# Low words of weights and folded weights: subtractions on the vector engine replaced by identity products in PSUM and by accumulating transfers

## The chip, the core and the metric

One core of a Trainium2 chip runs the whole program; the figure is device microseconds from a run's timing, and a profile of one execution gives every instruction's start and length. The core has a tensor engine (PE, matrix products into PSUM; PEld is its weight load), a vector engine (DVE), a scalar engine (ACT), GpSimd (POOL) and SyncE (SP); SP and POOL issue the DMA transfers here.

## The reference, cut to what matters

```python
a = softmax(phi over the sequence)               # per head, 576 tokens x 32 memories
k_m = a^T k ; v_m = a^T v                        # 32 x 64 per head
attn = softmax(q k_m^T / 8) ; out = attn v_m     # 8 batches, 8 heads, 64 columns a head
x = out, heads side by side                      # 4608 x 512
h = x @ w_in ; r = max(h, 0) ; y = (r * r) @ w_out   # w_in 512 x 2048, w_out 2048 x 512
```

The data is float32 and the products must keep more digits than one reduced product does. So the kernel writes each operand as a high word that the tensor engine takes in one pass (type float32r) and a low word, the rest, and sums three products: high by high, high by low, low by high.

## The kernel before, in words

**Work.** A batch has 576 tokens: 512 "main" ones in four blocks of 128, and 64 left over. `memory` makes the 32 memories of four heads, `scores` and `attention` make the attention weights `ath`, `atl` (high and low). The values are not multiplied by the attention weights first: `vw_alone` (first pair of batches, 16 calls) and `vw_step` (later pairs) fold the memories' values into 256 columns of `w_in`, and the result, split again into high and low, is the tile `V` (row names vw). `mm1` then makes h for 128 hidden columns of one batch (12 products in two PSUM tiles), squares the positive part into `gh` and `glo` (high and low); `mm2` multiplies these by `w_out` (12 products of 512 columns into the four `acc` tiles). One call of `mm1` and one of `mm2` is a step; there are 128 steps, numbered in `seq`: the first 32 take batch 0, 1, 1 and 0 by eights, then batches 2 to 7 follow with 16 each. `mm2_left` does the tokens left over, once per pair of batches.

**Weights.** They come as float32. `decode` loads 256 KB pieces (`raw`, 16 of `w_in` called wi, 16 of `w_out` called wo), takes the two halves of each float apart on the vector engine, and puts the high part and the low part into a pair of words: L320 to L325 prepare `W` (the coarse value) and `T` (the rest, scaled), L326 adds them, a copy (a helper's line, L258, on ACT or DVE) makes the high word, L335 subtracts it from the sum to make the low word. Pieces of `w_in` are also stored to HBM (L339) and loaded again later (`wi_again`).

**Folded weights.** In `vw_alone`, 12 products (L468) fill one PSUM bank with the fold, a copy takes the high word (ACT or DVE), and L476 on the vector engine subtracts it from PSUM for the low word. The bank has one tile (tag `pv`).

**Order.** Every operation is recorded with an estimated cost for each engine that may do it, and `Plan.order` plays a list schedule with these costs: it decides which engine takes an operation that has two, and in which order each engine's instructions stand. The order is fixed when the program is built; at run time an engine takes its instructions strictly in it and waits where an input is late. Transfers are issued on SP (loads) and POOL (stores of the first six batches and of `w_in`).

Of the kernel before, what the change touches and what calls it, by code (L numbers as in the profile page):

```python
# [11 lines left out]
F32 = mybir.dt.float32  # L12
# [7 lines left out]
P = 128  # L20
# [4 lines left out]

STEP = 5200
LEAD = 9000

# [22 lines left out]
class Plan:  # L51
# [57 lines left out]
    def order(self):  # L109
        for o in reversed(self.ops):  # L110
            cost = min(o.ways.values()) + o.lat + o.size / 180.0 + (1800 if o.size else 0)
            late = min((u.late for u in o.users), default=1e9)
            if o.cap is not None:
                late = min(late, o.cap)
            o.late = late - cost
# [17 lines left out]
        while len(out) < len(self.ops):  # L133
# [38 lines left out]
            if o.size:  # L172
                wire = max(wire, t + 600) + o.size / 180.0
                o.end = wire + 1400
            out.append(o)
# [9 lines left out]
def tt(n):  # L185
    return 110 + 1.04 * n


def ts(n):
    return 110 + 0.52 * n  # L190


def act(n):
    return 120 + 0.86 * n
# [10 lines left out]
def tile_attention_moe(  # L205
# [63 lines left out]
    ident = sb.tile([P, P], F32, tag="ident", name="ident", bufs=1)  # L269
    make_identity(nc, ident)  # L270
    ones = sb.tile([P, 1], F32, tag="ones", name="ones", bufs=1)
    nc.vector.memset(ones, 1.0)
# [30 lines left out]
    def decode(kind, j, h, room):  # L303
# [15 lines left out]

        vec({"DVE": 560}, lambda e: nc.vector.tensor_scalar(tf(), high().bitcast(F32), TOP, -TOP, ALU.min, ALU.max), [rk], [tk], lead=True)  # L320
        op({"ACT": act(ND)}, lambda e: nc.scalar.activation(tf(), tf(), AF.Copy, scale=2.0 ** -112), [tk], [tk], lead=True)
        vec({"DVE": ts(ND)}, lambda e: nc.vector.tensor_scalar(W(), high(), SIGN, None, ALU.bitwise_and), [rk], [wk], lead=True)
        vec({"DVE": tt(ND)}, lambda e: nc.vector.scalar_tensor_tensor(W(), T(), 3, W(), ALU.logical_shift_left, ALU.bitwise_or), [tk, wk], [wk], lead=True)
        vec({"DVE": ts(ND)}, lambda e: nc.vector.tensor_scalar(T(), W(), POWER, None, ALU.bitwise_and), [wk], [tk], lead=True)
        vec({"DVE": tt(ND)}, lambda e: nc.vector.scalar_tensor_tensor(tf(), low(), 2.0 ** -52, tf(), ALU.mult, ALU.mult), [rk, tk], [tk], lead=True)  # L325
        vec({"DVE": tt(ND)}, lambda e: ENG[e].tensor_add(wf(), wf(), tf()), [tk, wk], [wk], lead=True)  # L326
        if kind == "wi":
            t = wi[0, j, 0, h] = st([P, 2, 2, SL], F32R, "wi", f"wi0_{j}_{h}", 3)
            part = lambda x: t()[:, x].rearrange("p c f -> p (c f)")
        else:  # L330
            t = wo[2 * j + h] = st([P, 2, DM], F32R, f"W{j}{'ab'[h]}", f"wo{j}{h}")
            part = lambda x: t()[:, x]
        k0, k1 = ((t, (h, x) if kind == "wi" else x) for x in (0, 1))
        op({"ACT": act(ND), "DVE": ts(ND)}, lambda e: copy(e, part(0), wf()), [wk], [k0], lead=True, port={"DVE": True})
        vec({"DVE": tt(ND)}, lambda e: ENG[e].tensor_sub(part(1), wf(), part(0).bitcast(F32)),  # L335
            [wk, k0], [k1], lead=True)
        if kind == "wi":
# [121 lines left out]
    def vw_alone(s, bp):  # L459

        ts_ = [wi[0, s, bp if s < 4 else 0, hh] for hh in (0, 1)]
        vh, vl = VT[bp]
        pw = pt("pv", f"pvw0_{s}_{bp}")

        def mm(e, hh):
            for i, (l, r) in enumerate(((vh, 0), (vh, 1), (vl, 0))):
                for x in (0, 1):
                    nc.tensor.matmul(pw()[:, hh * SL:(hh + 1) * SL], l()[:, 2 * hh + x, :], ts_[hh]()[:, r, x, :],  # L468
                                     start=(i == 0 and x == 0), stop=(i == 2 and x == 1))

        for hh in (0, 1):
            op({"PE": 720}, lambda e, hh=hh: mm(e, hh), [ts_[hh], vh, vl], [pw], lead=True, lat=300)
        V = VW[bp, s]
        part = lambda x: V()[:, x].rearrange("p h f -> p (h f)")
        op({"ACT": act(2 * SL), "DVE": tt(2 * SL)}, lambda e: copy(e, part(0), pw()), [pw], [(V, 0)], lead=True)
        vec({"DVE": tt(2 * SL)}, lambda e: nc.vector.tensor_sub(part(1), pw(), part(0).bitcast(F32)), [pw, (V, 0)], [(V, 1)], port=None, lead=True)  # L476

# [97 lines left out]
    def mm1(g):  # L575
# [11 lines left out]
        for h in (0, 1):  # L587
            cs = TOK[h]
            n = cs.stop - cs.start
            p = pt("h", f"h{g}_{h}", 2)  # L590

            def mm(e, cs=cs, n=n, p=p):
                i = 0
                for l, x in ((0, ah), (0, al), (1, ah)):
                    for hh in (0, 1):
                        nc.tensor.matmul(p()[:, 0:n], V()[:, l, hh, c0:c0 + P], x()[:, hh, cs], start=(i == 0), stop=(i == 5))  # L596
                        i += 1

            op({"PE": 6 * (n * 0.4167 + 11)}, mm, [V] + [(x, (hh, h)) for x in (ah, al) for hh in (0, 1)], [p], lat=300)
            op({"ACT": act(n) - 30, "DVE": tt(n)}, lambda e, cs=cs, n=n, p=p: nc.scalar.activation(r()[:, cs], p()[:, 0:n], AF.Relu) if e == "ACT"  # L600
               else nc.vector.tensor_scalar(r()[:, cs], p()[:, 0:n], 0.0, None, ALU.max), [p], [(r, h)])  # L601
        op({"ACT": act(SM)}, lambda e: nc.scalar.activation(gh(), r()[:, 0:SM], AF.Square), [r], [gh])  # L602
        op({"ACT": act(LEFT)}, lambda e: nc.scalar.activation(G()[:, 0, lc], r()[:, SM:S], AF.Square), [r], [(G, (b % 2, 0))])  # L603
        op({"ACT": act(S), "DVE": tt(S)}, lambda e: nc.scalar.activation(r(), r(), AF.Square) if e == "ACT"  # L604
           else nc.vector.tensor_mul(r(), r(), r()), [r], [r], port=BOTH)  # L605
# [102 lines left out]
    memory(0, 1, ("W4a", "W5a"))  # L708
    attention(0, True)
    for j in range(4):  # L710
# [76 lines left out]
```

## Time and profile before

| what | value |
|---|---|
| median of 3 runs | 840.82 us (840.16 to 842.5) |
| profiled execution | 842.42 us, of which 840.7 us from first to last instruction |
| PE busy | 770.8 us (92%), granted clock 0.983 on average |
| DVE busy | 607.8 us (72%) |
| ACT busy | 352.0 us (42%) |
| POOL busy | 55.1 us (7%) |

Shares of the whole span mix stages: the first 230 us carry all 32 decoded pieces and 16 folds beside 24 steps; the rest has no decoding. A busy PE is not a PE at its peak, since a product's length in the trace is more than the distance to the next product's start when they follow each other.

### The profile page before, as it was taken

Reading aid. Unit: us, or ns where it says so; the run is one execution under the profiler, and the core shown is the slowest. Engines: PE = TensorE matmul, PEld = TensorE weight load, DVE = VectorE, ACT = ScalarE, POOL = GpSimd, SP = SyncE. Lnnn points to the kernel's source line nnn. Section 1 sums busy time; section 2 is a strip of 40 time slices with the busy share of each in tenths; the row PEclk is TensorE's granted clock in tenths of the full one; section 3 lists DMA queues with packets and bytes.
Section 4 is the critical chain, followed back from the end, with each engine's and each line's share of the span. In section 5 each row is a group of like instructions: output and inputs, shape, how many; then the busy total and the mean of one; then the engine's idle time right before and its main releaser. Section 6 shows DMA issues by size and latency. Waiting matters only on the chain. (4 is left out here: it accounts for less than half of the span.)

```text
span 840.7 us, 12898 instructions
## 1 busy us (share of the span) xinstructions
PE 770.8 (92%) x4756; PEld 646.7 (77%) x4756; DVE 607.8 (72%) x1346; ACT 352.0 (42%) x819; POOL 55.1 (7%) x91
## 2 busy tenths in 40 slices
PE   3468669999969999999999999999999999999995
PEld 2246558989758788888888788888888888888884
DVE  3889999999747886686788656686869566784540
ACT  1234446556324344453334434553335344542320
POOL 3102110221000010001000100001000100000000
PEclk9999989999989999999999999999999999999998
DMA  7847673546563753332344433322532433100001
GB/s 218 231 136 236 184 217 128 176 151 204 149 149 98 190 125 101 106 102 51 100 136 105 129 110 101 114 68 51 142 84 56 125 114 101 54 14 37 1 1 62
DMA packets 91073, 97.87 MB, mean 116 GB/s; under 512 B 24644, under 2 KB 77892, under 8 KB 91012
## 3 DMA queue, kind: packets, MB, share of 16 engines
q1 hardware_dynamic: 80292, 81.55, 33.5%
q0 software_dynamic: 10720, 15.52, 7.0%
q8 instruction: 37, 0.61, 0.3%
q14 instruction: 24, 0.20, 0.1%
HBM read 79.17 MB, written 17.83 MB: 115 GB/s over the span
## 5 line engine op out<-in xcount | busy, mean ns | idle before, releaser
L596 PE MATMUL h<-ath,vw 128*128 128x320 f32 (+1 forms) x1024 | 215.3, 304 | 11.9 <-ACT r L600 6.3
L626 PE MATMUL acc<-wo,gh 128*128 128x512 f32 x512 | 206.7, 404 | 0.1
L627 PE MATMUL acc<-wo,gh 128*128 128x512 f32 x512 | 204.2, 399 | 0.0
L596 PEld LDWEIGHTS h<-ath,vw 128*128 128x128 f32 x1024 | 173.7, 193 | 28.5 <-ACT r L600 8.4
L629 PE MATMUL acc<-wo,glo 128*128 128x512 f32 x512 | 160.7, 407 | 2.9 <-DVE glo L606 2.4
L496 DVE TENSOR_TENSOR vw<-pvw,vw 64x256 fp32r<-64x256 f32 x192 | 78.6, 420 | 66.9 <-ACT vw L258 65.2
L258 ACT CAST vw<-pvw 64x256 fp32r<-64x256 f32 (+1 forms) x205 | 74.8, 380 | 104.0 <-PE pvw L487 65.2
L626 PEld LDWEIGHTS acc<-wo,gh 128*128 128x128 f32 x512 | 98.1, 192 | 20.6 <-ACT gh L602 1.5
L596 PE MATMUL h<-atl,vw 128*128 128x320 f32 (+1 forms) x512 | 112.8, 301 | 0.2
L627 PEld LDWEIGHTS acc<-wo,gh 128*128 128x128 f32 x512 | 98.2, 192 | 18.3
L601 DVE TENSOR_SCALAR r<-h 128x320 f32<-128x320 f32 (+1 forms) x142 | 65.0, 459 | 63.0 <-PE h L596 61.5
L629 PEld LDWEIGHTS acc<-wo,glo 128*128 128x128 f32 x512 | 89.6, 189 | 23.9 <-DVE glo L606 9.2
L602 ACT ACTIVATE gh<-r 128x512 fp32r<-128x512 f32 x128 | 80.8, 631 | 51.5 <-DVE r L601 39.1
L606 DVE TENSOR_TENSOR glo<-r,gh 128x512 fp32r<-128x512 f32 x128 | 87.5, 684 | 3.4 <-ACT r L604 1.8
L596 PEld LDWEIGHTS h<-atl,vw 128*128 128x128 f32 x512 | 84.4, 193 | 1.5 <-DVE atl L563 1.3
L600 ACT ACTIVATE r<-h 128x256 f32<-128x256 f32 (+1 forms) x114 | 45.4, 401 | 66.7 <-PE h L596 62.7
L603 ACT ACTIVATE gl<-r 128x64 fp32r<-128x64 f32 x128 | 32.5, 254 | 82.8 <-DVE r L601 81.0
L605 DVE TENSOR_TENSOR r<-r 128x576 f32<-128x576 f32 x59 | 44.5, 755 | 13.7 <-ACT gh L602 12.6
L652 PE MATMUL accl<-wo,gl 128*128 128x512 f32 x192 | 52.1, 396 | 0.1
L604 ACT ACTIVATE r<-r 128x576 f32<-128x576 f32 x69 | 47.2, 684 | 1.5
L525 PE MATMUL psc<-qT,kb 128*128 128x256 f32 (+1 forms) x128 | 41.3, 449 | 5.8 <-DVE S L529 2.7
L652 PEld LDWEIGHTS accl<-wo,gl 128*128 128x128 f32 x192 | 34.7, 188 | 7.7 <-DVE o L258 0.9
(97 smaller groups left out, 829.1 us busy)
## 6 DMA issues: line engine op xcount, KB each, us to landing
wi<-w_in_hi SPq DMA_DIRECT2D x56, 256.0 KB
wi<-w_in_lo SPq DMA_DIRECT2D x56, 256.0 KB
q<-in_q_dram SPq DMA_DIRECT2D x32, 288.0 KB
KV<-in_k_dram SPq DMA_DIRECT2D x32, 256.0 KB
KV<-in_v_dram SPq DMA_DIRECT2D x32, 256.0 KB
raw<-in_moe_w_in_dram SPq DMA_DIRECT2D x16, 512.0 KB
raw<-in_moe_w_out_dram SPq DMA_DIRECT2D x16, 512.0 KB
out_dram<-o POOLq DMA_DIRECT2D x20, 256.0 KB, 8.1
```

Of the source, the lines that this page charges most:

```text
L258: nc.scalar.copy(o, i) if e == "ACT" else ENG[e].tensor_copy(o, i)
L496: vec({"DVE": tt(SL)}, lambda e, V=V, pr=pr, src=src: nc.vector.tensor_sub(V()[pr, 1, hh, :], src(), V()[pr, 0, hh, :].bitcast(F32)), [pw, ...
L596: nc.tensor.matmul(p()[:, 0:n], V()[:, l, hh, c0:c0 + P], x()[:, hh, cs], start=(i == 0), stop=(i == 5))
L600: op({"ACT": act(n) - 30, "DVE": tt(n)}, lambda e, cs=cs, n=n, p=p: nc.scalar.activation(r()[:, cs], p()[:, 0:n], AF.Relu) if e == "ACT" e ...
L601: else nc.vector.tensor_scalar(r()[:, cs], p()[:, 0:n], 0.0, None, ALU.max), [p], [(r, h)])
L602: op({"ACT": act(SM)}, lambda e: nc.scalar.activation(gh(), r()[:, 0:SM], AF.Square), [r], [gh])
L604: op({"ACT": act(S), "DVE": tt(S)}, lambda e: nc.scalar.activation(r(), r(), AF.Square) if e == "ACT" else nc.vector.tensor_mul(r(), r(), ...
L606: vec({"DVE": tt(SM)}, lambda e: nc.vector.tensor_sub(glo(), r()[:, 0:SM], gh().bitcast(F32)), [r, gh], [glo])
L626: nc.tensor.matmul(a(), gh()[:, c], t()[:, 0], start=f0, stop=False)
L627: nc.tensor.matmul(a(), gh()[:, c], t()[:, 1], start=False, stop=False)
L629: nc.tensor.matmul(a(), glo()[:, c], t()[:, 0], start=False, stop=f1)
L652: nc.tensor.matmul(a(), G()[:, l, :], t()[:, w], start=(ff == 0 and n == 0), stop=(ff == NFF - 1 and n == 2))
```

## The change

In three places a subtraction or an addition of 128 x 512 leaves the vector engine.

- **Early pieces** (`by_pe`: both kinds for j below 2, and wi for j 2 and 3; 12 pieces). Addition and subtraction go. The scaled rest is written, negated, into the low word's place; the tensor engine sums W, minus the high word, minus that negated rest in a PSUM tile (`pd`, tag `pv`) by three products with the identity or its negative; ACT copies the sum to the low word.
- **Other wo pieces** (`late`, 12 pieces). The addition goes: the low word is W minus its high word, and a transfer issued on POOL adds T onto it in place. The other 8 wi pieces keep both.
- **Folds** (16). The subtraction goes: the tensor engine adds minus the high word to the same bank, and ACT copies the low word.

The high copies of pieces and folds may now only be on ACT, as may the positive part and the full square of batches 0 and 1 (DVE could take them before). The attention of batch 0 is no longer made in two halves. The planner's figures change: vector instructions 40 ns dearer, transfers 240 instead of 180 bytes per ns, landing on POOL 4000 ns.

```diff
+LANDS = {"SP": 1400, "POOL": 4000}
+WIRE = 240.0
-                wire = max(wire, t + 600) + o.size / 180.0
-                o.end = wire + 1400
+                wire = max(wire, t + 600) + o.size / WIRE
+                o.end = wire + LANDS[e]
 def tt(n):
-    return 110 + 1.04 * n
+    return 150 + 1.04 * n
...
+    minus = sb.tile([P, P], F32R, tag="minus", name="minus", bufs=1)
+    nc.scalar.activation(minus, ident, AF.Copy, scale=-1.0)
...
-        vec({"DVE": tt(ND)}, lambda e: nc.vector.scalar_tensor_tensor(tf(), low(), 2.0 ** -52, tf(), ALU.mult, ALU.mult), [rk, tk], [tk], lead=True)
-        vec({"DVE": tt(ND)}, lambda e: ENG[e].tensor_add(wf(), wf(), tf()), [tk, wk], [wk], lead=True)
...
-        op({"ACT": act(ND), "DVE": ts(ND)}, lambda e: copy(e, part(0), wf()), [wk], [k0], lead=True, port={"DVE": True})
-        vec({"DVE": tt(ND)}, lambda e: ENG[e].tensor_sub(part(1), wf(), part(0).bitcast(F32)),
-            [wk, k0], [k1], lead=True)
+
+        by_pe = j < 2 or kind == "wi" and j < 4
+        late = kind == "wo" and not by_pe
+        if by_pe:
+            vec({"DVE": tt(ND)}, lambda e: nc.vector.scalar_tensor_tensor(part(1), low(), -2.0 ** -52, tf(), ALU.mult, ALU.mult), [rk, tk], [k1], lead=True)
+        else:
+            vec({"DVE": tt(ND)}, lambda e: nc.vector.scalar_tensor_tensor(tf(), low(), 2.0 ** -52, tf(), ALU.mult, ALU.mult), [rk, tk], [tk], lead=True)
+            if not late:
+                vec({"DVE": tt(ND)}, lambda e: nc.vector.tensor_add(wf(), wf(), tf()), [tk, wk], [wk], lead=True)
+        op({"ACT": act(ND)}, lambda e: copy(e, part(0), wf()), [wk], [k0], lead=True)
+        if by_pe:
+            pd = pt("pv", f"pd{j}_{h}")
+
+            def mm(e):
+                nc.tensor.matmul(pd(), ident, wf(), start=True, stop=False)
+                nc.tensor.matmul(pd(), minus, part(0), start=False, stop=False)
+                nc.tensor.matmul(pd(), minus, part(1), start=False, stop=True)
+
+            op({"PE": 1400}, mm, [wk, k1, k0], [pd], lead=True, lat=300)
+            op({"ACT": act(ND) - 30}, lambda e: nc.scalar.copy(part(1), pd()), [pd], [k1], lead=True)
+        else:
+            vec({"DVE": tt(ND)}, lambda e: nc.vector.tensor_sub(part(1), wf(), part(0).bitcast(F32)),
+                [wk, k0], [k1], lead=True)
+        if late:
+
+            dma(lambda d: d(out=part(1), in_=tf(), accum_op=ALU.add), 4096 * P, [tk, k1], [k1], eng="POOL", lead=True)
...
-        op({"ACT": act(2 * SL), "DVE": tt(2 * SL)}, lambda e: copy(e, part(0), pw()), [pw], [(V, 0)], lead=True)
-        vec({"DVE": tt(2 * SL)}, lambda e: nc.vector.tensor_sub(part(1), pw(), part(0).bitcast(F32)), [pw, (V, 0)], [(V, 1)], port=None, lead=True)
+        op({"ACT": act(2 * SL)}, lambda e: copy(e, part(0), pw()), [pw], [(V, 0)], lead=True)
+        op({"PE": 240}, lambda e: nc.tensor.matmul(pw(), minus, part(0), start=False, stop=True, skip_group_check=True), [(V, 0)], [pw], lead=True, lat=300)
+        op({"ACT": act(2 * SL)}, lambda e: copy(e, part(1), pw()), [pw], [(V, 1)], lead=True)
...
-    attention(0, True)
+    attention(0)
```

How the built programs differ, at three places (a row is line, operation, output, inputs, shape; names carry their number, wi0_2_0 is the first half of piece 2 of `w_in`). First the vector engine around the correction words glo0 and glo1 of the first two steps, before the change; it decodes wo10, wo11 (scratch work_584) and wi0_2_0 (scratch work_646) there:

```order
L606 TENSOR_TENSOR glo0_657<-r0_437,gh0_475 128x512
L388 TENSOR_REDUCE mc1_1_659<-pmx1_1_655 128x1
L335 TENSOR_TENSOR wo10_651<-work_561,wo10_651 128x512
L323 SCALAR_TENSOR_TENSOR work_646<-work_646 128x512
L390 TENSOR_TENSOR phi1_1_258<-phi1_1_258,pmx1_1_655 128x640
L324 TENSOR_SCALAR work_646<-work_646 128x512
L326 TENSOR_TENSOR work_584<-work_584 128x512
L325 SCALAR_TENSOR_TENSOR work_646<-raw_563,work_646 128x512
L606 TENSOR_TENSOR glo1_704<-r1_449,gh1_532 128x512
L326 TENSOR_TENSOR work_646<-work_646 128x512
L335 TENSOR_TENSOR wo11_702<-work_584,wo11_702 128x512
```

And the changed program around glo0. Its lines L324 to L328 are those that were L320 to L324; L340 writes the negated rest straight into the low word's place of wi0_2_0 and wi0_2_1:

```order
L328 TENSOR_SCALAR work_540<-work_540 128x512
L324 TENSOR_SCALAR work_638<-raw_516 128x512
L340 SCALAR_TENSOR_TENSOR wi0_2_0_625<-raw_453,work_540 128x512
L413 TENSOR_REDUCE mc1_1_653<-pmx1_1_640 128x1
L326 TENSOR_SCALAR work_638<-raw_516 128x512
L324 TENSOR_SCALAR work_664<-raw_588 128x512
L327 SCALAR_TENSOR_TENSOR work_638<-work_638 128x512
L415 TENSOR_TENSOR phi1_1_278<-phi1_1_278,pmx1_1_640 128x640
L632 TENSOR_TENSOR glo0_680<-r0_584,gh0_642 128x512
L328 TENSOR_SCALAR work_638<-work_638 128x512
L326 TENSOR_SCALAR work_664<-raw_588 128x512
L340 SCALAR_TENSOR_TENSOR wi0_2_1_678<-raw_516,work_638 128x512
```

The four rows of addition (old L326) and subtraction (old L335) in the first fence have no counterpart, and wo10 and wo11, still in work beside glo0 before, are past it.

Second the tensor engine where the changed program folds this piece (pvw0_2_0 is the bank of the fold, vw0_0_2 its high word, minus the negated identity, acc0_0 the four tiles of `mm2`):

```order
L493 MATMUL pvw0_2_0_785<-wi0_2_1_678,VTh00_84 128x256 x4
L493 MATMUL pvw0_2_0_785<-wi0_2_1_678,VTl00_89 128x256 x2
L652 MATMUL acc0_0_3_690<-wo01_377,gh1_682 128x512
L653 MATMUL acc0_0_3_690<-wo01_377,gh1_682 128x512
L655 MATMUL acc0_0_0_657<-wo01_377,glo1_726 128x512
L655 MATMUL acc0_0_1_666<-wo01_377,glo1_726 128x512
L622 MATMUL h2_1_827<-atl0_395,vw0_0_1_510 128x320
L622 MATMUL h2_1_827<-ath0_392,vw0_0_1_510 128x320 x2
L501 MATMUL pvw0_2_0_785<-vw0_0_2_819,minus_68 128x512
L463 MATMUL pvt1_1_840<-ident_63,vx1_1_803 128x128
```

The product L501, which waits for ACT's copy of the high word, stands six rows (seven products) behind the fold's last product L493; before the change the tensor engine had no row for a fold's low word.

Third GpSimd's queue, the changed program, from the first accumulating transfer (L361; L364 are the stores of `w_in` that were L339):

```order
L361 DMA wo20_728<-work_664 128x512
L364 DMA w_in_hi_78<-wi0_3_0_825 128x2x256
L361 DMA wo21_772<-work_735 128x512
L364 DMA w_in_lo_79<-wi0_3_0_825 128x2x256
L364 DMA w_in_hi_78<-wi0_3_1_881 128x2x256
L364 DMA w_in_lo_79<-wi0_3_1_881 128x2x256
L361 DMA wo30_944<-work_912 128x512
L361 DMA wo31_1014<-work_939 128x512
```

The transfers for wo20 to wo31, used by steps 4 to 7, stand between the stores of `w_in`; before, only those stores stood there.

## Rows read from the trace of the kernel before

**Rows 1.** The page, the span in 40 slices, tenths busy.
```profile
PE   3468669999969999999999999999999999999995
...
DVE  3889999999747886686788656686869566784540
```
**Rows 2.** Windows: busy us of each engine in five stretches.
```profile
core 0: us, PE busy (x) PEld busy (x) DVE busy (x) ACT busy (x) POOL busy (x), PEclk, DMA share, GB/s
...
0.00:60.00 60.00, 27.66 (x212) 17.03 (x212) 40.27 (x101) 14.18 (x28) 10.82 (x21) 1.00 0.69 201
60.00:130.00 70.00, 53.77 (x366) 41.34 (x367) 65.27 (x145) 33.04 (x72) 9.61 (x14) 0.90 0.64 196
...
130.00:225.70 95.70, 93.54 (x586) 82.27 (x584) 88.97 (x180) 56.09 (x118) 12.00 (x16) 1.00 0.54 167
225.70:306.30 80.60, 73.52 (x484) 59.69 (x481) 58.78 (x132) 28.41 (x73) 7.69 (x14) 0.96 0.59 146
306.30:818.00 511.70, 509.66 (x3064) 436.67 (x3063) 352.51 (x788) 219.24 (x529) 14.95 (x26) 1.00 0.30 84
```
**Rows 3.** Timeline, PE: first correction products of steps 4, 5, 22 and 32.
```profile
117.82 0.50 PE L629 MATMUL acc<-wo,glo 128*128 128x512 f32 x1 [0.94 <-DVE glo L606]
...
129.96 1.08 PE L629 MATMUL acc<-wo,glo 128*128 128x512 f32 x4
...
225.67 1.20 PE L629 MATMUL acc<-wo,glo 128*128 128x512 f32 x4
...
306.32 0.84 PE L629 MATMUL acc<-wo,glo 128*128 128x512 f32 x3
```
**Rows 4.** Timeline, DVE: 512-column instructions in a row (start us, length us).
```profile
169.05 0.68 DVE L258 CAST vw<-pvw 128x512 fp32r<-128x512 f32 x1
169.65 0.68 DVE L606 TENSOR_TENSOR glo<-r,gh 128x512 fp32r<-128x512 f32 x1
```
**Rows 5.** Waits to 226 us: waiting line, releaser, us, times, longest.
```profile
DVE mx L384 <- DMA phi<-in_phi_dram: 6.9, 2, 3.9
...
DVE work L320 <- DMA raw<-in_moe_w_in_dram: 1.5, 1, 1.5
...
SPq L318 <- DVE work L325: 47.5, 11, 9.1
```
**Rows 6.** The chain that ended last, late stretch: start us, us, what.
```profile
657.57 0.88 PE h L596 x6
...
660.62 0.72 PE h L596 x6
...
684.19 0.23 PE acc L627
...
703.89 0.72 PE pvw L487 x6
...
719.87 0.86 PE psc L525 x4
```
**Rows 7.** Timeline, 42 us: ACT copies a fold, PE waits for it.
```profile
42.08 0.59 ACT L258 CAST vw<-pvw 128x512 fp32r<-128x512 f32 x1 [2.54 <-PE pvw L468]
...
42.72 0.58 PE L596 MATMUL h<-ath,vw 128*128 128x256 f32 x1 [0.68 <-ACT vw L258]
```
**Rows 8.** POOL's stores: L339 (ns min/median/max, landing), page's output stores (last: landing).
```profile
L339 POOL DMA_DIRECT2D w_in_lo<-wi x16: 725/727/1122, 39.8 to 204.1; - x16
...
DMA to landing us min/median/max: 2.6/3.7/5.5
...
out_dram<-o POOLq DMA_DIRECT2D x20, 256.0 KB, 8.1
```
**Rows 9.** Timeline near 241 us: DVE and PE after a long wait.
```profile
241.68 1.23 DVE L384 TENSOR_REDUCE mx<-phi 128x128 f32<-128x640 f32 x1 [6.66 <-DMA phi<-in_phi_dram]
...
245.55 0.47 PE L438 MATMUL pvt<-ident,vx 128*128 128x128 f32 x1 [5.91 <-DVE vx L434]
```

More of the change, by code (lines that the diff above doesn't have):

```diff
@@ L110, in order @@
         for o in reversed(self.ops):
-            cost = min(o.ways.values()) + o.lat + o.size / 180.0 + (1800 if o.size else 0)
+            cost = min(o.ways.values()) + o.lat + o.size / WIRE + (1800 if o.size else 0)
             late = min((u.late for u in o.users), default=1e9)
@@ L185, in tt @@
 def tt(n):
-    return 110 + 1.04 * n
+    return 150 + 1.04 * n
 def ts(n):
-    return 110 + 0.52 * n
+    return 150 + 0.52 * n
 def act(n):
@@ L318, in decode @@
         dma(lambda d: d(R().rearrange("p (c f t) -> p c f t", c=src.shape[1], t=2), src), 4096 * P, w=[rk], lead=True)
-        vec({"DVE": 560}, lambda e: nc.vector.tensor_scalar(tf(), high().bitcast(F32), TOP, -TOP, ALU.min, ALU.max), [rk], [tk], lead=True)
+        vec({"DVE": ts(ND)}, lambda e: nc.vector.tensor_scalar(tf(), high().bitcast(F32), TOP, -TOP, ALU.min, ALU.max), [rk], [tk], lead=True)
         op({"ACT": act(ND)}, lambda e: nc.scalar.activation(tf(), tf(), AF.Copy, scale=2.0 ** -112), [tk], [tk], lead=True)
@@ L468, in mm @@
                     nc.tensor.matmul(pw()[:, hh * SL:(hh + 1) * SL], l()[:, 2 * hh + x, :], ts_[hh]()[:, r, x, :],
-                                     start=(i == 0 and x == 0), stop=(i == 2 and x == 1))
+                                     start=(i == 0 and x == 0 and hh == 0), stop=(i == 2 and x == 1), skip_group_check=True)
         for hh in (0, 1):
@@ L599, in mm1 @@
             op({"PE": 6 * (n * 0.4167 + 11)}, mm, [V] + [(x, (hh, h)) for x in (ah, al) for hh in (0, 1)], [p], lat=300)
-            op({"ACT": act(n) - 30, "DVE": tt(n)}, lambda e, cs=cs, n=n, p=p: nc.scalar.activation(r()[:, cs], p()[:, 0:n], AF.Relu) if e == "ACT"
+            op({"ACT": act(n) - 30, **({} if b < 2 else {"DVE": tt(n)})}, lambda e, cs=cs, n=n, p=p: nc.scalar.activation(r()[:, cs], p()[:, 0:n], AF.Relu) if e == "ACT"
                else nc.vector.tensor_scalar(r()[:, cs], p()[:, 0:n], 0.0, None, ALU.max), [p], [(r, h)])
@@ L603, in mm1 @@
         op({"ACT": act(LEFT)}, lambda e: nc.scalar.activation(G()[:, 0, lc], r()[:, SM:S], AF.Square), [r], [(G, (b % 2, 0))])
-        op({"ACT": act(S), "DVE": tt(S)}, lambda e: nc.scalar.activation(r(), r(), AF.Square) if e == "ACT"
+        op({"ACT": act(S), **({} if b < 2 else {"DVE": tt(S)})}, lambda e: nc.scalar.activation(r(), r(), AF.Square) if e == "ACT"
            else nc.vector.tensor_mul(r(), r(), r()), [r], [r], port=BOTH)
```

## The prediction

> **What bounds the kernel now.** I read the slices first: PE is full from about the seventh slice on with dents, DVE from the fourth to the tenth [rows 1]. An average hides which of the two ends last, so I cut the span at steps, where the first correction product of a step starts: step 4 at 117.82 us, step 5 at 129.96, step 22 at 225.67, step 32 at 306.32 [rows 3]. The windows between these cuts [rows 2] show four regimes. Until 60 us DVE works 40.3 us and the transfer engines 0.69 of the time. From 60 to 130 us DVE is busy 65.3 of 70 us while PE works 53.8: the decoding holds the kernel, and step 4's correction product waits for DVE's glo [rows 3]. From 130 to 225.7 both are near full (PE 93.5, DVE 89.0 of 95.7). From 306 on PE is busy 509.7 of 511.7 us and DVE has a third free. So a microsecond taken off DVE counts before 130 us, and later only where PE is waiting.
>
> Are the loads behind it? DVE waits 6.9 us for the memories' phi and 1.5 us for pieces of w_in until 226 us, while SP's loads of pieces wait 47.5 us for DVE (L325) to free the raw buffers [rows 5]. The loads follow DVE, not DVE the loads.
>
> **The change part by part.** DVE first. Instructions of 512 columns last 0.68 us, but in a full queue start 0.60 us apart (169.05, 169.65) [rows 4]; 0.60 is the price of one removed. In the two orders, up to the correction word of step 4, the changed program has 15 additions fewer, 8 subtractions for wi, 2 for wo and 4 for folds: 29 x 0.60 = 17.4 us. The other differences (batch 0's attention in one piece, a few instructions that stand elsewhere) cancel to 0.3 us by their lengths, and I take none. If DVE still paces that stretch, step 4's mark comes at 117.8 - 17.4 = **100.4 us**. The lower end for this gain is 0 (another pace-maker), the upper 17.4.
>
> PE's new work. The trace has no 512-column product of plain float32; the nearest row is psc, two float32 products of 256 columns in 0.86 us, so one of 512 is 0.86 us [rows 6]. A reduced 512-column product is 0.23 us [rows 6]. An early piece costs 0.86 + 2 x 0.23 = 1.32 us, 12 pieces 15.8 us; the 16 folds 16 x 0.23 = 3.7 us; together 19.5 us. In the order all 12 pieces and 4 folds stand ahead of step 4: 16.8 us. PE stands idle 32.3 us before 60 and 16.2 us from there to 130 [rows 2], 48.5 us, which cover them; without the cover they would count in full. By the Trainium skill (Trainium Kernel Development and Optimization, section Performance Expectations) matmul busy time misjudges how full PE is, and LDWEIGHTS busy is the better measure. In 60 to 130 us the weight loads are busy 41.3 of 70 us against 436.7 of 511.7 later [rows 2], 59% against 85%, so by it the cover is wider than the idle time says: at the later density 41.3 us of loads need 48.4 us, which leaves 21.6 us instead of 16.2. The sum stays as it is by either.
>
> ACT gets 12 copies from `pd`, a second one for each of the 16 folds, and what DVE can no longer take. At 0.59 us a copy [rows 7] the 28 are 16.5 us; ACT is busy 103 of 225.7 us [rows 2] and covers them.
>
> The new waits. A fold's identity product waits for ACT's high copy, and the next user of the single `pv` bank for the low copy; an early piece's bank waits for one copy. That is 2 x 16 + 12 = 44 hand-overs from PE to ACT and back. Where nothing lies between, one costs PE 0.68 us [rows 7], and behind PE's waiting row stand its own next rows, `mm1` and `mm2` products, so everything waits. The order puts other products between; in the quoted place seven, over 1 us. The ends are 0 and 44 x 0.68 = 29.9 us. I take 4 bare ones, in the start where PE has little to put between: **2.7 us**. The constants of the planner and the relu and squares that move to ACT change only orders; I price them at nothing, because PE is what lasts, with the range holding the rest.
>
> The accumulating transfers. Only wo20 to wo31 are needed soon (steps 4 to 7). The subtraction of wo20 stands two rows behind glo1 on DVE, so about three steps lie between. A step costs PE 12 x 0.23 + 0.88 + 0.72 = 4.36 us [rows 6], three 13 us. No row shows an accumulating transfer; the bounds are POOL's stores, which issue in 0.73 us and land in 3.7 (w_in), or at 8.1 (output, the farthest) [rows 8]. Even 8.8 us is inside 13, so I take 0; with no lead it would be 4 x 8.8 = 35 us. A rule speaks against it: the Trainium skill (SBUF — State Buffer, the paragraph on the "DVE blocks DMA" trap) says that while DVE runs a two-port operation, GpSimd can't write descriptors for its transfers, so that they start late. Here POOL issued 32 stores of w_in beside a full DVE with a median of 0.727 us and a maximum of 1.122 [rows 8]: 0.4 us at worst, so the trace does not bear it out.
>
> **From step 4 to the end.** Counting PE's rows between the marks in the changed order: 228 products of 512 columns, 114 of 320, 258 of 256 and little else, 228 x 0.23 + 114 x 0.147 + 258 x 0.12 + 0.5 = 100.7 us (0.88 / 6 and 0.72 / 6 a product). The old order has, between steps 5 and 22, 204 of 512, 102 of 320 and 234 of 256, by the same prices 90.3 us with the small ones, and took 95.7 us: a factor 1.06. So the changed stretch takes 106.7 us, and step 22 comes at 100.4 + 2.7 + 106.7 = 209.8 instead of 225.7. From there to step 32 the changed order holds 3.8 us less on PE (12 products of 320 and 24 of 256 moved ahead, 2 psc added): 80.6 - 4.0 = 76.6, step 32 at 286.4, 19.9 earlier. In this stretch DVE stood 6.66 us before a phi transfer and PE 5.91 us behind it [rows 9]; I let that wait stand, between 0 and 5.9 us of gain. After step 32 PE has 0.6 us more to do and no idle time to give back. Sum: 19.9 - 0.6 = 19.3 us, a span of 821.4; with 1.7 us around the span 823.1. The profiled execution, 842.4, stands 1.6 above the median of 840.8, so in terms of the median **821.5 us**.
>
> **The rivals.**
> - Forecast: DVE's relief brings the PE-bound stretch forward, 812 to 829 us. Chance 0.60.
> - More: all hand-overs are hidden (2.7), and the wait at 241 us goes as DVE has more room (5.9), 821.5 - 8.6 = 813, and down to some 804 if as much again of the gaps before 130 us closes. For it: up to step 22 DVE's order is 73 instructions shorter, and the sum uses 29. Against: that wait was for a transfer. Chance 0.17.
> - The loads hold the start: transfers are busy 0.69 in the first 60 us [rows 2], and 12 transfers are added. Half the relief lost gives 830, all of it 821.5 + 17.4 = 839: then the change doesn't do what it says for the time, since DVE was not the bound. Against it [rows 5]. Chance 0.10.
> - Hand-overs bare, the other side: the bank `pv` is single, and PE stands for ACT at most of the 44. Each further one costs 0.68 us; from 33 bare ones on the 19.3 + 2.7 us are gone and it decides, at 44 the time is 821.5 + 40 x 0.68 = 849. Against it: the products put between. Chance 0.07.
> - The accumulating transfers land late. Four transfers, each up to 4 us (half of 8.1 [rows 8]) beyond its lead, with PE in front of L653: 821.5 + 16 = 837. The Trainium skill's paragraph on the "DVE blocks DMA" trap (SBUF — State Buffer) would bring it about. Against it [rows 8]. Chance 0.06.
>
> **How the numbers follow.** The likeliest case gives 821.5 us, its own range 812 to 829. The range for 8 in 10 goes from 804 to 836: below it almost nothing is left, above it most of the hand-over case, the late transfers and the worse half of the load case, some 0.16. A measurement of this kernel tells 0.3% (2.5 us) from no change. Faster by more: 0.60 + 0.17 + 0.05 of the load case + 0.06 (late transfers) = 0.88. Within: 0.05, the load case at its end. Slower: 0.07, the hand-overs.
>
> **What would show it.** Right: step 4's mark near 100 to 104 us, step 22's near 205 to 213, DVE below 85% between them while PE stays above 95%; psc-like pd products of 0.86 us; L653 waiting for no transfer. Wrong: step 4 later than 110 us (then the term of 17.4 fails, and DVE or the loads show why); PE waits for ACT's L260 or L355 of more than 10 us in sum; waits of PE for L361; or an interval from step 32 to the end that differs from 534 us by more than 3.

## The result, and the profile after

The changed kernel takes 830.1 us in the median of four runs (828.47 to 831.64), the kernel before 841.66 (840.16 to 846.77): a ratio of 0.985 [0.982, 0.989], faster by 11.6 us. The forecast was 821.5 us, some 20 below the kernel before. The sign was right, and the time lies in the range given for 8 in 10 (804 to 836), 1.1 us outside that of the likeliest case (812 to 829); 8.6 us to the forecast are missing. The profiled execution took 829.28 us, with a span of 827.6.

The page's busy times and slices of the changed kernel, to hold against [rows 1]:

```profile
PE 777.8 (94%) x4820; PEld 650.1 (79%) x4820; DVE 547.2 (66%) x1224; ACT 396.4 (48%) x904; POOL 65.1 (8%) x103
...
PE   4679998899979999999999999999999999999995
...
DVE  3888997484447856786768465786778555874540
```

DVE lost 60.6 us of work (607.8 before), and PE is dense three slices earlier. But the PE row has two 8s, from 124 to 166 us, where [rows 1] has 9s. The marks say what they cost. The changed kernel's timeline, the first correction products (now L655) of steps 4, 22 and 32:

```profile
102.32 1.10 PE L655 MATMUL acc<-wo,glo 128*128 128x512 f32 x3
...
218.29 0.62 PE L655 MATMUL acc<-wo,glo 128*128 128x512 f32 x2
...
292.69 1.08 PE L655 MATMUL acc<-wo,glo 128*128 128x512 f32 x4
```

Against [rows 3], step 4 comes 15.5 us earlier, step 22 only 7.4, step 32 13.6, and the end 13.1. So the gain was there at step 4 and half of it was lost between steps 4 and 22. The windows cut at these marks, with the columns of [rows 2]:

```profile
0.00:60.00 60.00, 36.18 (x325) 21.26 (x326) 41.73 (x96) 22.73 (x42) 13.96 (x26) 0.94 0.84 245
60.00:102.30 42.30, 40.54 (x280) 32.24 (x279) 39.13 (x93) 28.01 (x64) 9.89 (x13) 1.00 0.92 263
102.30:218.30 116.00, 108.57 (x647) 94.86 (x646) 77.90 (x164) 73.34 (x158) 19.23 (x25) 0.96 0.59 165
```

Two things are to be seen. From 60 us to step 4 PE is busy 40.54 of 42.30 us: the idle time that was to cover the new products is used up there. Whether PE then sets the pace beside DVE the windows don't tell; e1, e6 and e11 below speak against it. Between steps 4 and 22 DVE has 38 us free and PE still stands 7.4 us, at a granted clock of 0.96. The waits of PE in that stretch (waiting line, releaser, us in sum, times, longest):

```profile
PE pvw L501 <- ACT vw L260: 4.0, 1, 4.0
PE acc L655 <- DVE glo L632: 3.1, 2, 2.5
```

No transfer is named, and L653 waits for nothing. The timeline around the 4.0 us shows what stands behind ACT's copy:

```profile
144.89 1.81 POOL L361 DMA_DIRECT2D wo<-work  x2 [6.30 <-DVE work L342]
...
150.85 0.40 PE L655 MATMUL acc<-wo,glo 128*128 128x512 f32 x1
152.85 0.43 DVE L324 TENSOR_SCALAR work<-raw 128x512 f32<-128x512 f32 x1 [5.29 <-DMA wo<-work]
153.31 1.39 ACT L325 ACTIVATE work<-work 128x512 f32<-128x512 f32 x2 [4.43 <-DVE work L324]
154.60 0.57 ACT L260 CAST vw<-pvw 128x512 fp32r<-128x512 f32 x1
155.22 0.80 PE L501 MATMUL pvw<-vw,minus 128*128 128x512 f32 x1 [3.98 <-ACT vw L260]
```

This is read from the bottom up. PE's identity product for a fold waits for ACT's copy; ACT's queue stood behind L325 of the next piece; that waits for DVE's L324, the piece's first write into the scratch `work`; and L324 waits 5.29 us for a transfer `wo<-work` to finish with that scratch. Two were issued together (144.89, x2), the halves of one piece of w_out, and the two halves of the next piece are to be written into their places: the first L324 (152.85) starts when the first has landed, 7.88 us after its issue, the second (153.60) when the second has. The chain of work (what released each instruction, followed back from the last) up to 230 us shows the second of them, and one more (start us, us, what):

```profile
145.52 8.00 DMA wo<-work
154.06 0.63 ACT work L325
154.69 0.48 ACT vw L260
155.22 0.80 PE pvw L501
...
191.91 8.04 DMA wo<-work
200.43 0.60 SPq L378
```

Both take 8 us. The one at 191.91 has a similar follower: it belongs to the last piece, whose scratch is a place of the keys and values, so SP's loads of these, and the load of q behind them in SP's queue, wait for it, and DVE's L546 then waits 8.7 us for q; PE has work there and loses only 0.55 us (207.97).

The hole at 151 us costs more than its idle time. Windows over it:

```profile
151.30:155.20 3.90, 0.00 (x0) 0.00 (x0) 2.35 (x6) 1.77 (x4) 0.26 (x1) 0.93 0.24 68
155.20:161.70 6.50, 6.48 (x21) 5.51 (x22) 4.92 (x11) 2.42 (x6) 0.52 (x1) 0.52 0.58 185
161.70:190.00 28.30, 28.21 (x167) 24.90 (x167) 23.50 (x48) 21.58 (x46) 8.65 (x11) 1.00 0.59 164
```

After PE stood 3.98 us the granted clock is 0.52 for 6.5 us, near the 1.2 GHz level, with PE full. The timeline, PE, shows products of 512 columns first 0.43 and then 0.24 us apart:

```profile
157.09 0.63 PE L652 MATMUL acc<-wo,gh 128*128 128x512 f32 x1
157.52 0.63 PE L653 MATMUL acc<-wo,gh 128*128 128x512 f32 x1
...
161.88 0.40 PE L652 MATMUL acc<-wo,gh 128*128 128x512 f32 x1
162.12 0.39 PE L653 MATMUL acc<-wo,gh 128*128 128x512 f32 x1
```

At the full clock the 6.48 us of work would have been some 3.4 (an estimate: 6.48 x 0.52), so the clock takes 3.1 us and the hole 7.1 in all. There is another of 2.54 us, up to 130.5 (PE for DVE's glo, behind a 4.7 us wait of L324 for a load of w_in), and a low clock follows it too:

```profile
130.00:135.00 5.00, 4.48 (x19) 4.10 (x20) 4.93 (x11) 3.15 (x8) 1.51 (x2) 0.66 0.48 111
```

That is some 1.5 us by the same estimate. So of the 116.0 us 7.4 are idle, 4.6 go to the clock, and 104.0 are work at the full clock; the forecast had 106.7.

DVE's waits to 230 us, against [rows 5]:

```profile
DVE qT L546 <- DMA q<-in_q_dram: 11.0, 2, 8.7
...
DVE work L324 <- DMA raw<-in_moe_w_in_dram: 7.4, 4, 4.7
DVE mx L409 <- DMA phi<-in_phi_dram: 6.7, 2, 3.7
DVE work L324 <- DMA wo<-work: 5.3, 1, 5.3
```

The pieces' loads of w_in now keep DVE waiting 7.4 us instead of 1.5, the wait for q was 0.6 us before, and the one for `work` is new.

### The profile page after: what moved, and what is told of

Its sections match the earlier page's. It is cut to its first block, busy times and chain, and to the rows that moved or that the text cites. A ratio compares the mean times of both kernels' runs of the same rounds, so it can differ in the third digit from the quotient of the medians.

```text
span 827.6 us, 13055 instructions
## 1 busy us (share of the span) xinstructions
PE 777.8 (94%) x4820; PEld 650.1 (79%) x4820; DVE 547.2 (66%) x1224; ACT 396.4 (48%) x904; POOL 65.1 (8%) x103
## 4 chain that ended last, share of the span: by engine, by line
PE 69%; DVE 11%; DMA 9%; issue 4%; ACT 4%; SPq 1%; POOL 1%; DVEq 0%; ACTq 0%; POOLq 0%
PE h L622 19%; PE acc L655 12%; PE acc L652 11%; PE acc L653 11%; PE accl L678 5%; PE pvw L513 4%; DMA raw<-in_moe_w_in_dram 3%; PE psc L551 2%; PE pkv L426 2%; DMA wo<-work 2%; DMA phi<-in_phi_dram 2%; ACT vw L260 1%; DMA q<-in_q_dram 1%; DMA raw<-in_moe_w_out_dram 1%; DVE glo L632 1%
## 5 line engine op out<-in xcount | busy, mean ns | idle before, releaser
L622 PE MATMUL h<-ath,vw 128*128 128x320 f32 (+1 forms) x1024 | 211.9, 299 | 1.5 <-DVE ath L260 1.3
L653 PE MATMUL acc<-wo,gh 128*128 128x512 f32 x512 | 202.1, 395 | 0.0
L655 PE MATMUL acc<-wo,glo 128*128 128x512 f32 x512 | 163.7, 412 | 3.5 <-DVE glo L632 3.3
L260 ACT CAST vw<-pvw 64x256 fp32r<-64x256 f32 (+1 forms) x224 | 85.8, 397 | 94.5 <-PE pvw L513 47.1
L522 DVE TENSOR_TENSOR vw<-pvw,vw 64x256 fp32r<-64x256 f32 x192 | 78.7, 420 | 73.5 <-ACT vw L260 71.7
L652 PEld LDWEIGHTS acc<-wo,gh 128*128 128x128 f32 x512 | 96.8, 189 | 21.0 <-issue 2.2
L622 PE MATMUL h<-atl,vw 128*128 128x320 f32 (+1 forms) x512 | 110.7, 296 | 0.2
L655 PEld LDWEIGHTS acc<-wo,glo 128*128 128x128 f32 x512 | 91.0, 191 | 24.1 <-DVE glo L632 10.1
L653 PEld LDWEIGHTS acc<-wo,gh 128*128 128x128 f32 x512 | 96.8, 189 | 16.5
L626 ACT ACTIVATE r<-h 128x256 f32<-128x256 f32 (+1 forms) x146 | 58.8, 405 | 64.9 <-PE h L622 63.8
L627 DVE TENSOR_SCALAR r<-h 128x320 f32<-128x320 f32 (+1 forms) x110 | 50.3, 459 | 56.3 <-PE h L622 55.7
L630 ACT ACTIVATE r<-r 128x576 f32<-128x576 f32 x99 | 67.8, 685 | 2.4
L551 PE MATMUL psc<-qT,kb 128*128 128x256 f32 (+1 forms) x128 | 37.8, 415 | 1.6 <-DVE S L555 1.4
L513 PE MATMUL pvw<-wi,VTh 128*128 128x256 f32 x192 | 37.6, 288 | 0.3 <-DVE vw L522 0.3
```

Source lines behind the costliest of these rows:

```text
L260: nc.scalar.copy(o, i) if e == "ACT" else ENG[e].tensor_copy(o, i)
L513: nc.tensor.matmul(pw()[:, x * SL:(x + 1) * SL], l()[:, 2 * hh + x, :], w(r, x), start=(i == 0), stop=(i == 2))
L522: vec({"DVE": tt(SL)}, lambda e, V=V, pr=pr, src=src: nc.vector.tensor_sub(V()[pr, 1, hh, :], src(), V()[pr, 0, hh, :].bitcast(F32)), [pw, ...
L626: op({"ACT": act(n) - 30, **({} if b < 2 else {"DVE": tt(n)})}, lambda e, cs=cs, n=n, p=p: nc.scalar.activation(r()[:, cs], p()[:, 0:n], A ...
L630: op({"ACT": act(S), **({} if b < 2 else {"DVE": tt(S)})}, lambda e: nc.scalar.activation(r(), r(), AF.Square) if e == "ACT" else nc.vecto ...
L652: nc.tensor.matmul(a(), gh()[:, c], t()[:, 0], start=f0, stop=False)
```

## The experiments

Step marks are starts of a step's first correction product in the trace; span and PE busy are from the page, idle is their difference; all four come from the one profiled execution. In e7 and e9 that one stood 4.6 and 4.8 us above the median, so their marks may be late by as much; in the others it is within 1.7. All are in us; ratios are to the kernel before, run again beside each of the three groups of experiments (medians 842.03, 842.07 and 842.34).

| kernel | median | ratio [95%] | step 4 | step 22 | span | PE busy | PE idle |
|---|---|---|---|---|---|---|---|
| before | 841.66 | 1 | 117.8 | 225.7 | 840.7 | 770.8 | 69.9 |
| changed | 830.10 | 0.985 [0.982, 0.989] | 102.3 | 218.3 | 827.6 | 777.8 | 49.8 |
| e1_no_acc | 820.93 | 0.975 [0.973, 0.977] | 103.8 | 207.7 | 819.6 | 775.7 | 43.9 |
| e2_plain | 825.85 | 0.981 [0.979, 0.984] | 103.0 | 213.9 | 823.7 | 776.8 | 46.9 |
| e3_late_234 | 823.69 | 0.979 [0.976, 0.982] | 103.4 | 209.1 | 820.3 | 773.4 | 46.9 |
| e4_lands8 | 832.44 | 0.988 [0.986, 0.991] | 103.4 | 224.4 | 832.3 | 783.4 | 48.9 |
| e5_pieces_only | 816.82 | 0.970 [0.967, 0.973] | 104.6 | 208.6 | 815.0 | 771.9 | 43.1 |
| e6_folds_only | 830.18 | 0.985 [0.982, 0.988] | 110.3 | 216.8 | 829.0 | 765.7 | 63.3 |
| e7_neither | 827.85 | 0.984 [0.980, 0.987] | 111.7 | 219.2 | 830.8 | 767.9 | 62.9 |
| e8_old_figures | 828.74 | 0.983 [0.981, 0.986] | 100.2 | 204.8 | 825.5 | 778.7 | 46.8 |
| e9_figures_only | 842.07 | 1.000 [0.998, 1.002] | 118.3 | 230.0 | 844.8 | 775.5 | 69.3 |
| e10_act_only | 849.24 | 1.009 [1.008, 1.011] | 114.8 | 219.8 | 846.9 | 774.2 | 72.7 |
| e11_few_pieces | 826.21 | 0.983 [0.980, 0.986] | 109.8 | 215.5 | 824.0 | 773.3 | 50.7 |
| e12_split | 818.67 | 0.974 [0.971, 0.976] | 104.5 | 208.8 | 815.9 | 771.8 | 44.1 |

Theory A: the accumulating transfers hold scratch and take the missing gain. Theory B: loads that come late under the planner's new figures took it. Theory C: the hand-overs to ACT did. Runs one to four ask about the transfers, the others about the rest.

**e1_no_acc.** The 12 later pieces of w_out add on DVE again, nothing accumulates by transfer.

```diff
-        late = kind == "wo" and not by_pe
+        late = False
```

> Changed kernel, but the twelve later pieces of w_out get their addition back on DVE (L344) instead of the accumulating transfer. Theory A (the accumulating transfers, landing after some 6 to 8 us, hold the scratch of the pieces, so that DVE stands before a reused scratch and PE behind it): the 5.3 us wait of L324 on a transfer to wo goes, DVE gets 12 x 0.60 = 7.2 us more in a stretch where it is busy 77.9 of 116 us, steps 4 to 22 take 107 to 111 us instead of 116.0, the time is 822 to 826 us. Theory B (loads that come late under the new planner figures are what was lost): steps 4 to 22 stay at 114 to 118, time 828 to 833. Theory C (hand-overs to ACT): the same as B.

820.93 us, 9.2 less than the changed kernel and 1 us more of a gain than Theory A had. Step 4 comes 1.5 us later (the additions are back on DVE), step 22 10.6 earlier: the stretch takes 103.9 us where 107 to 111 were expected. The windows of this kernel between those marks:

```profile
103.80:150.00 46.20, 45.24 (x266) 39.99 (x265) 44.70 (x96) 34.63 (x76) 4.37 (x6) 1.00 0.54 183
150.00:207.70 57.70, 57.54 (x404) 49.86 (x403) 47.35 (x100) 38.75 (x84) 7.75 (x12) 1.00 0.64 193
```

DVE has 14 us more work than in the changed kernel and costs nothing by it; PE is idle 1.1 us, and the clock is 1.00. The transfers took a load off an engine that had room, and the holes go with them, also the one behind the load of w_in: L324 waits 0.6 us for such loads between these marks, under the same planner's figures, so Theory B falls. How the transfers delay that load wasn't looked at further.

**e2_plain.** The same transfers in the same order, but copying.

```diff
-            dma(lambda d: d(out=part(1), in_=tf(), accum_op=ALU.add), 4096 * P, ...
+            dma(lambda d: d(out=part(1), in_=tf()), 4096 * P, ...
```

> Changed kernel with the same order of every instruction; the twelve transfers copy instead of accumulating, so the low words of those pieces lack their coarse part (that part of the computation is left out). If accumulating as such makes the landing long (Theory A1): the median landing falls from 6.3 to 4.8 us or less, as for the stores of w_in, and the time to 824 to 827. If a transfer from GpSimd's queue at that place lands so late whatever it does (A2): landing 5.8 to 6.8, time 828 to 832.

825.85 us, so 4 of the 9 us go with the accumulation and 5 stay with the transfer. The time is A1's; the landing is just above it. L361 in the changed kernel (ns min/median/max of an issue, and us to landing):

```profile
L361 POOL DMA_DIRECT2D wo<-work x12: 844/906/1177, 74.3 to 191.9; - x12
...
DMA to landing us min/median/max: 3.7/6.3/8.0
```

and in this one:

```profile
L361 POOL DMA_DIRECT2D wo<-work x12: 531/570/583, 75.6 to 188.4; - x12
...
DMA to landing us min/median/max: 2.7/4.9/6.3
```

The hole is the same one, 3.17 us of PE idle up to 153.02, behind a wait of 4.77 us of L324. A plain copy also holds the scratch. The other hole is shorter as well (1.3 us instead of 2.5).

**e3_late_234.** Only pieces 2, 3 and 4 accumulate by transfer.

```diff
-        late = kind == "wo" and not by_pe
+        late = kind == "wo" and 2 <= j < 5
```

> Changed kernel, but only the pieces 2, 3 and 4 of w_out are accumulated by transfers (there five scratch places stand in turn); pieces 5, 6 and 7, with four, two and two places, add on DVE. Theory A: the waits for wo near 145 to 153 and 192 to 200 us go, the gain is nearly that of leaving out all transfers, 823 to 827. Theories B and C: 828 to 832.

823.69 us, as Theory A had it: the transfers of pieces 5 to 7 carry 6.4 of the 9.2 us, roughly, since the four runs lie between 821.2 and 827.9. The hole at 151 us and the wait for q stand in their time; six transfers are left, the last at 122.7 us, and no instruction waits for them. The scratch has fewer places in the later pieces.

**e4_lands8.** The planner's figure for POOL's landing raised from 4 to 8 us, near what was measured.

```diff
-LANDS = {"SP": 1400, "POOL": 4000}
+LANDS = {"SP": 1400, "POOL": 8000}
```

> Changed kernel with the planner's landing on GpSimd at 8000 instead of 4000 ns, nothing else. Theory A: the planner now knows when the scratch is free and puts other work before the reuse, 822 to 827 us. Theories B and C: 828 to 832, the order around the transfers moves and nothing is won.

832.44 us, not better, against Theory A. The timeline of this kernel: the same chain, longer.

```profile
157.59 0.76 DVE L324 TENSOR_SCALAR work<-raw 128x512 f32<-128x512 f32 x2 [7.13 <-DMA wo<-work]
...
159.72 0.79 PE L501 MATMUL pvw<-vw,minus 128*128 128x512 f32 x1 [6.23 <-ACT vw L260]
```

A truer figure alone doesn't make room. That places of scratch are what lacks is read from e3; scratch of its own for the transfer wasn't tried, and that cure stays open.

**e5_pieces_only.** As e1, and the low words of the folds are subtracted on DVE again; only the early pieces are summed on PE.

```diff
-        op({"PE": 240}, lambda e: nc.tensor.matmul(pw(), minus, part(0), start=False, ...
-        op({"ACT": act(2 * SL)}, lambda e: copy(e, part(1), pw()), [pw], [(V, 1)], lead=True)
+        vec({"DVE": tt(2 * SL)}, lambda e: nc.vector.tensor_sub(part(1), pw(), part(0)...
```

> As the version without accumulating transfers (820.9 us), but a fold's low word is subtracted on DVE again (L476's way); so only the twelve early pieces use identity products. Theory of the prediction (a 512-column instruction taken off DVE is worth 0.60 us while DVE paces, that is ahead of step 4, and nothing later, where PE gets 0.23 us per fold back): 4 folds x 0.60 = 2.4 us later at step 4 (some 106 instead of 103.8), 12 x 0.23 = 2.8 us less on PE after it: 819 to 823 us. Rival (DVE still paces until step 22): 16 x 0.60 = 9.6 us, 828 to 831.

816.82 us, the fastest of all, 13.3 below the changed kernel and 2 below the range that was expected. The folds' identity products cost 4.1 us on top of e1: 3.8 more PE busy and 0.8 more idle in the table, where 16 x 0.23 = 3.7 was their price. They take work off DVE, and hardly anything comes of it: step 4 is 0.8 us earlier with them, step 22 0.9.

**e6_folds_only** has the folds' products without the pieces', **e7_neither** has neither, so that the planner's figures, the ACT-only copies, relu and squares and the undivided attention are left.

```diff
-        by_pe = j < 2 or kind == "wi" and j < 4
+        by_pe = False
```

> As the version without accumulating transfers, but no piece uses identity products (addition and subtraction of all 32 pieces on DVE); only the 16 folds do. Theory of the prediction: of the 29 instructions ahead of step 4 only the 4 folds are saved, step 4 near 115 us, 12 folds later help little: 833 to 839 us. Rival (the early pieces win little because their 15.8 us on PE take back what DVE gains): 821 to 828.

> The rest of the change alone: the planner's figures, copies, relu and squares of the first pair on ACT alone, attention of batch 0 in one piece; no identity products, no accumulating transfers. Theory of the prediction (these only move the order): 836 to 845 us, step 4 at 113 to 120. Rival (they carry the gain, since DVE loses the relu, squares and copies of the first 32 steps): 825 to 834.

830.18 and 827.85 us; e6 lies between both of its ranges, e7 in its rival's. The folds' products alone don't help, and the 2.3 us between the two are too few to tell. The pieces gain 11.0 us without the folds' products (e7 to e5) and 9.2 with them (e6 to e1); in the latter pair idle time falls by 19.4 us and PE's work rises by 10.0. The rest, priced at nothing, is worth 14.2 us (e7), more than the whole change brings. Added in the order rest, pieces (e5), folds (e1), transfers (the changed kernel), the parts are -14.2, -11.0, +4.1 and +9.2 us: the three that the change is named for give 2.3 us back together, and two of them lose. The windows of e6 to step 4:

```profile
0.00:60.00 60.00, 28.75 (x289) 18.48 (x290) 44.00 (x97) 15.82 (x28) 13.21 (x25) 0.84 0.77 227
60.00:110.30 50.30, 41.16 (x270) 32.60 (x269) 47.22 (x106) 27.64 (x60) 6.79 (x10) 0.92 0.72 230
```

DVE is busy 47.2 of 50.3 us and PE 41.2: without the pieces DVE is the fuller engine here, as the forecast said of the kernel before.

**e8_old_figures.** As e1, with the planner's old figures and the divided attention.

```diff
-LANDS = {"SP": 1400, "POOL": 4000}
-WIRE = 240.0
+LANDS = {"SP": 1400, "POOL": 1400}
+WIRE = 180.0
...
-    return 150 + 1.04 * n
+    return 110 + 1.04 * n
...
-    attention(0)
+    attention(0, True)
```

> The version without accumulating transfers with the planner's old figures (180 bytes per ns, vector instructions 40 ns cheaper) and batch 0's attention in two halves. Theory of the prediction (priced at nothing): 818 to 824 us. Rival (the new figures fit the engines and give a better order): 826 to 832.

One of the old figures isn't restored here, that for a piece's first instruction on DVE (560 ns before). The time is 828.74 us, as the rival had it, 7.8 more than e1, though steps 4 and 22 come earlier (100.2, 204.8). It is lost from step 22 to 33: 93.0 us against 80.9. PE is busy 83.3 us of it (75.1 in e1), so most of the difference is work that the plan puts there, and idle time is 9.7 against 5.8.

**e9_figures_only** is the kernel before with the new figures alone, **e10_act_only** the kernel before with only the engine choices taken from DVE (the diff shows one of the four places).

```diff
-        op({"ACT": act(ND), "DVE": ts(ND)}, lambda e: copy(e, part(0), wf()), ...
+        op({"ACT": act(ND)}, lambda e: copy(e, part(0), wf()), [wk], [k0], lead=True)
```

> The kernel before with the planner's new figures alone (vector instructions 40 ns dearer, 240 bytes per ns, landing on GpSimd 4000 ns). The rest of the change without products and transfers gave 827.9 us, 14 us under the kernel before. Theory P (a plan by other figures orders the first 300 us better): 828 to 834. Rival Q (it is the copies, relu and squares that only ACT may take, which free DVE): 838 to 844 here, the gain in the next run.

> The kernel before with only this: high copies of pieces and folds, and relu and full squares of batches 0 and 1, on ACT alone. Theory P: 838 to 844. Rival Q: 828 to 834, since before, 8 relus, 3 squares and 4 copies stood on DVE up to step 22 by the orders, about 7 us.

842.07 us, no change, and 849.24, 6.9 slower: rival Q for the first, neither theory for the second. Neither holds the 14 us of e7. In e10 the wait of [rows 9] is there, a little longer, in the timeline:

```profile
243.90 1.23 DVE L384 TENSOR_REDUCE mx<-phi 128x128 f32<-128x640 f32 x1 [7.86 <-DMA phi<-in_phi_dram]
...
245.78 1.22 PE L629 MATMUL acc<-wo,glo 128*128 128x512 f32 x2 [6.86 <-DVE glo L606]
```

A DVE instruction that waits for a load holds back glo, and PE stands for it.

**e11_few_pieces** is e5 with 8 pieces on PE rather than 12, **e12_split** is e5 with the divided attention.

```diff
-        by_pe = j < 2 or kind == "wi" and j < 4
+        by_pe = j < 2
```

```diff
-    attention(0)
+    attention(0, True)
```

> The version with identity products for early pieces alone (816.8 us), but for 8 pieces (j below 2) instead of 12. If PE paces from step 0 on as much as DVE (PE was busy 40.5 of 42.3 us between 60 us and step 4 in the changed kernel): 4 x 1.32 = 5.3 us off PE against 4 x 2 x 0.60 = 4.8 us more on DVE, 815 to 819 us. If DVE still paces there: 820 to 823. If PE alone does: 811 to 814.

> The version with identity products for early pieces alone (816.8 us), with batch 0's attention in two halves again. Priced at nothing: 815 to 819. Rival (one piece saves DVE 16 instructions and is a part of the rest's gain): 820 to 826.

826.21 and 818.67 us. Four pieces fewer cost 9.4 us, more than any of the three cases had: step 4 comes 5.2 later, for 8 instructions back on DVE (0.65 us each), and the rest is lost before step 33 as well. So nearly all that the pieces bring comes with these four; the first eight give 1.6 us (e7 to e11), too few to tell. The divided attention makes no difference that these runs can tell.

## Why the prediction came out as it did

**The number: luck.** By the parts above the forecast had 0 for the rest and 0 for the transfers, where -14.2 and +9.2 us were measured, and -19.3 for the pieces, the folds and the later additions on DVE, where the pieces and folds gave -6.9. These errors nearly cancel; the mechanism that the forecast rests on brought about a third of what it was to bring.

**DVE's 17.4 us before step 4: right in the sum, not in its parts.** Forecast with 2.7 us of hand-overs was 103.1, measured 102.3. But by the marks the rest of the change with the folds brings 7.5 us (117.8 to 110.3, e6; forecast 2.4 for the folds), the pieces 6.5 (to 103.8, e1) and the later additions 1.5. The folds' share is 0.8 (e5 to e1). Pieces and later additions are 25 of the 29 instructions, 15.0 us by the forecast, and gave 8.0. The errors cancelled. Of the signs that were named, step 4's mark fell where it should (100 to 104 us), step 22's not (205 to 213), and PE was busy 94% between them rather than above 95. The differences depend on the order in which the parts are added, as e9 and e10 show.

**The cover on PE: the second step that failed.** The price was right, as the changed kernel's timeline shows for one piece:

```profile
86.70 1.02 PE L350 MATMUL pd<-work,ident 128*128 128x512 f32 x2
...
87.16 0.80 PE L351 MATMUL pd<-wi,minus 128*128 128x512 f32 x1
...
87.80 0.39 PE L352 MATMUL pd<-wi,minus 128*128 128x512 f32 x1
```

From 86.70 to 87.80 and one product of 0.23 on are 1.33 us, against 1.32. That 48.5 us of idle time cover them, while every instruction off DVE gains 0.60 us, was wrong, and it went wrong at the start. The windows of e6 (no piece on PE), then of e1 (12 pieces), each up to the first correction product of step 0 and from there to step 4:

```profile
0.00:71.50 71.50, 37.84 (x337) 25.80 (x337) 54.40 (x122) 24.32 (x49) 13.94 (x26) 0.86 0.77 229
71.50:110.30 38.80, 32.07 (x221) 25.28 (x221) 36.82 (x82) 19.13 (x39) 6.07 (x9) 0.91 0.71 227
...
0.00:72.10 72.10, 48.29 (x371) 29.98 (x372) 50.52 (x115) 29.36 (x59) 15.41 (x28) 0.88 0.82 238
72.10:103.80 31.70, 30.32 (x223) 24.07 (x223) 28.87 (x68) 18.89 (x39) 4.94 (x8) 1.00 0.74 222
```

Ahead of step 0 DVE has 3.9 us less to do and the mark comes no earlier; from there to step 4 it has 8.0 us less and 7.1 are gained, although PE is busy 30.3 of 31.7 us. (e7 and e5 say the same: 71.6 and 71.7, then 40.1 and 32.9.) In the trace of the kernel before, 15 of the 29 instructions stand ahead of step 0, and [rows 2] had DVE busy only 40.3 of the first 60 us. Nor is PE's idle time there, 23.8 us in e1, a cover: the identity products are on e1's chain of work up to step 0, beside a load.

```profile
29.41 11.39 DMA raw<-in_moe_w_in_dram
42.77 2.08 PE pd L350 x2
...
60.17 1.76 PE pd L350 x2
...
63.09 1.12 PE pd L350 x2
```

Which of the two holds step 0 wasn't tested.

**Hand-overs.** PE's waits for ACT's L260 and L355 sum to some 7 us in the whole run, and the longest, 4.0, isn't a bare hand-over but the transfer's. Without it they are the 2.7 us of the forecast. The rival of 44 bare ones is out. That the loads hold the start has more for it than before, with the load on the chain above and transfers busy 0.92 of the time from 60 us to step 4 (0.75 in e1, which comes to step 4 no sooner). Its 830 us for half the relief is the measured time, but by chance: step 4 came at 102.3, so the relief was there.

**The accumulating transfers at 0: the step that failed.** It asked how long before L653 a transfer lands, found 13 us of lead, and was right in that: no product waits for one. It didn't ask who needs the transfer's source next. They landed at 6.3 us in the median and 8.0 at most, inside the 8.8 allowed, and what they cost is the next writer of the scratch. The runs put it at 9.2 us (e1), of which 4 are the accumulation's longer time (e2), and 6.4 belong to pieces 5 to 7 (e3). With it the forecast's 821.5 becomes 830.7, beside 830.1 measured, which is chance as well, since the other terms were off by more. The rival of late transfers had the culprit, at 16 us, but the wrong place. Why a transfer takes 8 us there and 3.7 elsewhere isn't settled: the transfer engines are busy 0.86 of the time while the one of 144.89 is under way, and 0.94 during the one of 3.7 us (at 171.4). The Trainium skill (SBUF — State Buffer, the paragraph on the "DVE blocks DMA" trap) would have GpSimd kept from writing a transfer's descriptors while DVE runs a two-port operation. The accumulating issues take at most 1.18 us, against 1.12 in [rows 8], and DVE stood still for the last 5.29 us of the transfer at 151 us; so the trace doesn't show that rule behind the 8 us.

**From step 32 to the end.** 534.9 us against 534 forecast. From step 36 on all 14 kernels agree within 1% (461.1 to 463.9 us to step 120). All that the change does it does before that.

**The planner's figures, the engine choices and the undivided attention at nothing: failed in size, though the forecast's range held it.** They are worth 14.2 us together on the kernel before, 0 and -6.9 for two of them alone, and 7.8 for figures and attention on top of e1. The attention alone gives 1.9 at most (e5, e12). So the 14 us come of the parts acting together, and the cause stays open. Of the 9.9 us that e7's profiled execution is ahead, 6.1 are there at step 4 and 3.5 come between steps 22 and 33 (79.8 us against 83.3). In e8 and e10 the loss lies in that second stretch (93.0 and 96.6 us): there their traces show a wait for a load [rows 9] and more work on PE, put there by the redrawn order; which choice of the planner makes it wasn't found. [rows 9]'s wait became shorter, 4.0 us of PE for L463 in two pieces against 5.91, within the bounds given for it.

## What to carry to other kernels

An engine's work that is moved to a transfer keeps its source occupied until the transfer has landed: look for who writes that place next, not only for who reads the result. Idle time of the second engine is no cover for work that stands on the chain, and relief of the first one counts only where that one sets the pace: here nothing ahead of step 0, and nine tenths from step 0 to step 4. And where a planner draws the order, a change of its figures alone can move the time by as much as the change under study, so such edits are to be run by themselves before a gain is put down to anything else.

## What the runs showed of the hardware

A 256 KB transfer within the core that accumulates took 6.3 us to land in the median and 8.0 at most, where the same transfer as a copy took 4.9 and 6.3; to issue it took POOL 0.906 us against 0.570. After 3.98 us without a product the granted clock was 0.52 for the next 6.5 us of full work, which adds three quarters of the idle time to its cost; after 2.54 us it was 0.66 over 5 us. And work given to PE while it has gaps cost less than its length: its busy time rose by 10.0 us where 12 x 1.33 = 16 us of products came in (e6 to e1), with the mean granted clock at 0.973 before and 0.981 after (0.92 and 0.98 from 60 us to step 4); that the clock explains it wasn't tested.
